# Block-sparse attention and a rational FFN in one pass: four chunks through half of the FFN's units first, and GpSimd's weight loads behind the keys

## The chip, the cores and the metric

The kernel runs on one core of one Trainium2 chip. The metric is the device time of one execution in microseconds (us); lower is better. Engines have the profile's names: PE (TensorE), PEld (its weight loads), DVE (VectorE), ACT (ScalarE), POOL (GpSimd), SP (SyncE, which only issues DMAs).

## What is computed

Four batches of 768 tokens, eight heads of 64, in float32. Attention is sparse by blocks of 32 tokens: a query block sees itself and its two neighbours, the first and the last block, and three sampled blocks; the first and the last query block see all. Its output, 3072 x 512, goes through an FFN whose activation is a rational function:

```python
mask = np.abs(blk_i - blk_j) <= window
mask = mask | (blk_i == 0) | (blk_j == 0) | (blk_i == n_blocks - 1) | (blk_j == n_blocks - 1)
...
attn = attn / (np.sum(attn, axis=-1, keepdims=True) + 1e-09)
...
h = x @ w_in
P = a[0] + a[1] * h + a[2] * h2 + a[3] * h3
Q = 1.0 + np.abs(b[0]) * np.abs(h) + np.abs(b[1]) * h2
g = P / (Q + 1e-06)
return (g @ w_out).astype(np.float32)
```

w_in (512 x 2048) and w_out (2048 x 512) come as 64-bit floats, which no engine computes with: the kernel loads them as pairs of 32-bit words and puts float32 together with integer operations.

## The kernel before, in words

**Chunks, units, parts.** The tokens are cut into 12 chunks of 256, three to a batch. A chunk's FFN has 8 units of 256 hidden features (`unit`, line 1017). A unit is 24 matmuls into hidden features (`into`, lines 1034 to 1036; weights as a float16 high and low half), three activations on ACT, seven operations on DVE that make the rational function (the one that makes its high half, `gh`, is line 1069), and 12 matmuls into the output accumulator (`out_high`, lines 1091 and 1093, and `out_low`, line 1097). Attention (`attention`, line 730) goes by pairs of query blocks, 12 pairs to a batch; the pair with the first and the last block is worked in three parts, so a batch has 14 parts. A part is a group of score matmuls (line 815), four maxima on DVE (827), four exponentials on ACT (846), eight transposes (892) and the products with the values (938). Two pairs make one transposed tile of FFN input (976), four pairs a chunk.

**Near scores.** Batch 0 takes its sampled key blocks out of SBUF: six GpSimd copies a pair (line 759). For that all six key tiles must have been loaded (579), transposed (554) and copied out of PSUM (592).

**Weights.** `weights` (396) loads w_in in 16 pieces of 512 KB (four groups of 512 columns, four pieces each, line 429) and w_out in 16 (426), and decodes each: a conversion on any of three engines, then three operations on DVE (438, 441, 444). A group of w_in also needs a scale, then a scaling and a split into halves; a piece of w_out is copied to `wo_h` (452), its remainder goes to `wo_l` (458), and a bfloat16 copy to `wo_b` (455). GpSimd issues groups 0 and 1 of w_in, SP the rest. Raw pieces of w_in lie in the parts of `wo_l` and `wo_b` that have no weights yet: four places a group (`raw`, 409).

**What sets the order.** Nothing is issued as it is recorded. Every step is an `Op` with an engine, a price, the Ops it waits for and a priority; `issue` (164) then plays a list schedule over the prices and writes one fixed order for each engine. Inside an engine the order is never changed on the chip. An Op may be placed only when its priority is at most 8 above the unit reached. A unit's priority is its place in `order` (393); attention's comes from `part_prio` (1160), a weight piece's from the place of the first unit that needs it. Where the planner sees PE idle at the start, it writes `fill` matmuls there (162), whose result nobody reads. In `order` chunk 0 goes through units 0 to 3, chunk 1 through all 8, then chunk 0 through 4 to 7, and from chunk 2 on each chunk through all 8. Chunk 0's half sum waits in SBUF, in a tile of the ring `r_ld`, and the second half is added to it (1135).

```python
    order = [(0, u) for u in range(HU)] + [(1, u) for u in range(NU)] + [(0, u) for u in range(HU, NU)] + [(c, u) for c in range(2, NC) for u in range(NU)]
```

Of the kernel before, what the change touches and what calls it, by code (L numbers as in the profile page):

```python
# [24 lines left out]
def kernel(  # L25
# [46 lines left out]
    PT = 3  # L72
# [307 lines left out]

    WC = 512
# [4 lines left out]
    wo_b = const.tile([P, NF, DM], BF16, name="wo_b")  # L386
# [6 lines left out]
    order = [(0, u) for u in range(HU)] + [(1, u) for u in range(NU)] + [(0, u) for u in range(HU, NU)] + [(c, u) for c in range(2, NC) for u in range(NU)]  # L393
    place = {cu: n for n, cu in enumerate(order)}

    def weights():
# [5 lines left out]
        for u in range(NG):  # L402
            pieces += [(min(place[0, 2 * u], place[1, 2 * u]) + -4.91, 0, u, x) for x in range(NCC)]
        for x in range(NF):
            pieces.append((min(place[0, x // 2], place[1, x // 2]) + x % 2 / 2 + 0.45, 1, x // NCC, x))
        pieces.sort(key=lambda p: p[0])
        sums, before, begun, freed = {}, [None, None], {}, {}

        def raw(u, x):
            x0 = (x // 2 if u == 0 else 2 + x // 2) * NCC  # L410
            home = [wo_l, wo_b][x % 2][:, x0:x0 + NCC]
            return home.rearrange("p a n -> p (a n)").bitcast(I32)

        def homes(x):
            x //= NCC
            return [freed[0 if x < 2 else NG - 1, 2 * (x % 2) + y] for y in range(2)]

        def one(prio, kind, u, x, before):
            d = {}
            s_wl = Slot(r_wl) if kind else None  # L420
# [39 lines left out]
            wl = [s_wl] if kind else []  # L460
# [6 lines left out]
            o = Op(among("c", SC, sc=520, po=588, ve=335), 0, convert, [o0], prio, takes=w, uses=wl)  # L467
            if not kind:
                begun[u, x] = o
# [5 lines left out]
            if kind:  # L475
                o1 = Op(among("o", SC, sc=520, po=588, ve=335), 0, out_high, [o], prio, uses=w)
                o2 = Op(among("p", PO, po=1225, ve=602), 0, out_low, [o1] + homes(x), prio, uses=w)
                o3 = Op(among("q", SC, sc=520, po=588, ve=335), 0, out_short, [o] + homes(x), prio, uses=w)
                out_ready[x] = [o2, o3]
                decoded.append(o3)  # L480
                decoded.append(o2)
                return o2
# [43 lines left out]
    kall = const.tile([P, NB, HG, BLK], F32, name="kall")  # L526
# [36 lines left out]
    def new_ld(slot):  # L563
        return slot.buf.tile([P, 512], F32, name="ld", bufs=4 if ext and slot.buf is ext[0] else None)
# [44 lines left out]
    def prep(b, when):  # L609
# [9 lines left out]
        def tile_of(w, j):  # L619
            if not first:  # L620
                slot = Slot(r_ld)
                return slot, lambda: new_ld(slot)
            ring, tag, pool = homes[j // 2]
            return Slot(ring), lambda: pool.tile([P, 512], F32, name=tag, bufs={"tt": 3}.get(tag))
# [101 lines left out]
    xbufs = [[const.tile([P, CB, NCC, BLK], F16, name=f"{nm}{e}") for nm in ("xh", "xl")] for e in range(3)]  # L726
# [290 lines left out]
    def unit(c, u):  # L1017

        b, k0 = c // NCH, place[c, u]
        new, last = u == 0 or (c == 0 and u == HU), u == NU - 1 or (c == 0 and u == HU - 1)  # L1020
# [78 lines left out]
        deps = (o_ready[c] + [o_fc[b, u]] if u == 0 else [o_fc[b, u]]) + (in_ready[u * CH // WC] if c < 2 else [])  # L1099
# [17 lines left out]
        wo = out_ready[2 * u] + out_ready[2 * u + 1] if c < 2 else []  # L1117
# [42 lines left out]
    def part_prio(x):  # L1160

        c = next(c for c in range(NC) if x < need[c])
        if c == 0:
            return -19.0 + 1.78 * x
        since, by = place[c - 1, 0], place[c, 0]
        if c == 2:
            since = 9.1
        if c == 1:
            return by + (0.56 * (x + 1 - need[1])) - 1
# [74 lines left out]
```

## Time and profile before

| | |
|---|---|
| three runs | 827.95, 831.24, 833.78 us; median 831.24 |
| the profiled execution | 831.69 us, of which 829.9 us from the first to the last instruction (the span) |
| busy share of the span | PE 93%, DVE 81%, ACT 69%, POOL 12% |
| mean granted clock of PE | 0.981 |
| DMA | 121.30 MB, mean 146 GB/s |

A row of a group has the line, engine, operation, tiles, shapes and count, then the busy time of the group in us, the mean of one in ns, and the idle time of its engine just before it with what ended that. Busy times of matmul groups overlap each other, since each matmul's end is modelled. A granted clock of 1.00 is 2.4 GHz, 0.50 is 1.2 GHz. "issue" as a releaser is a wait whose end the profile can't put down to another instruction.

### The profile page before, as it was taken

To read this page: it belongs to the slowest core of one execution; us is meant where nothing else is said; L and a number is where in the kernel's file an instruction comes from. 1 tells how busy PE (TensorE), PEld (TensorE's weight loads), DVE (VectorE), ACT (ScalarE), POOL (GpSimd) and SP (SyncE) were. 2 spreads that over 40 slices of the span, in tenths; PEclk is the share of its full clock that TensorE was granted. 3 is DMA by queue.
4 is the path that set the end of the run, shared out by engine and by line. 5 is a ranking of instruction groups with operands and counts; after the bars stand their busy time and mean duration, and the time that the engine had idled before them with its cause. 6 is when DMAs were issued, how large, how long until landed. Compare 5 with 4: busy or idle time off the path is not lost.

```text
span 829.9 us, 27531 instructions
## 1 busy us (share of the span) xinstructions
PE 776.0 (93%) x10935; PEld 556.8 (67%) x10935; DVE 673.1 (81%) x1579; ACT 569.9 (69%) x1266; POOL 99.4 (12%) x147
## 2 busy tenths in 40 slices
PE   4997937799899999999999999999999999999997
PEld 2655625676677768677777777677777767767774
DVE  2777899899988985788888884887888886887886
ACT  1775676788777768767576759676676758766563
POOL 1747344533100000000000000000000000000000
PEclk9998977899999999999999999999999999999999
DMA  7877673449555866545536756625556436210000
GB/s 209 239 220 230 193 224 114 138 120 248 154 153 159 203 171 180 166 128 167 147 108 173 188 145 191 181 83 172 149 140 151 116 106 183 77 62 6 1 26 26
DMA packets 224417, 121.30 MB, mean 146 GB/s; under 512 B 62624, under 2 KB 214048, under 8 KB 224288
## 3 DMA queue, kind: packets, MB, share of 16 engines
q1 hardware_dynamic: 223136, 115.34, 50.1%
q0 software_dynamic: 1152, 4.19, 1.4%
q8 instruction: 86, 1.41, 0.7%
q14 instruction: 43, 0.35, 0.1%
HBM read 108.47 MB, written 11.01 MB: 144 GB/s over the span
## 4 chain that ended last, share of the span: by engine, by line
PE 81%; DVE 11%; ACT 3%; issue 3%; SPq 2%; DMA 1%; POOL 0%; ACTq 0%; DVEq 0%
PE acc L1091 10%; PE acc L1093 9%; PE acc L1097 9%; PE ph L1034 9%; PE ph L1035 9%; PE ph L1036 9%; PE m L815 7%; PE av L938 6%; PE m L892 6%; PE acc L162 3%; PE m L554 2%; SPq L579 2%; PE m L976 1%; DVE pr L827 1%; DVE dw L444 1%
## 5 line engine op out<-in xcount | busy, mean ns | idle before, releaser
L1034 PE MATMUL ph<-xh,wi 128*128 128x256 f16 x768 | 210.7, 274 | 1.1 <-DVE tt L1051 1.1
L1035 PE MATMUL ph<-xl,wi 128*128 128x256 f16 x768 | 210.3, 274 | 0.0
L1036 PE MATMUL ph<-xh,wi 128*128 128x256 f16 x768 | 210.3, 274 | 0.0
L1041 ACT ACTIVATE sq<-ph,fc 128x512 f32<-128x512 f32 x96 | 65.9, 686 | 113.4 <-PE ph L1036 113.3
L1091 PE MATMUL acc<-wo_h,gh 128*128 128x512 f32 x384 | 114.4, 420 | 15.5 <-DVE gh L1069 14.8
L846 ACT ACTIVATE pr<-pr,st 128x256 f32<-128x256 f32 x224 | 110.7, 500 | 8.5 <-DVE st L858 8.4
L1058 DVE SCALAR_TENSOR_TENSOR ab<-sq,absb,ab 128x512 f32<-128x512 f32 x96 | 75.6, 787 | 39.0 <-ACT ab L1055 38.5
L1097 PE MATMUL acc<-wo_b,gl 128*128 128x512 bf16 x384 | 99.3, 381 | 4.1 <-DVE gl L1079 4.1
L1093 PE MATMUL acc<-wo_l,gh 128*128 128x512 bf16 x384 | 100.5, 385 | 0.0
L827 DVE CUSTOM_DVE_ANT_1 pr<-m,bias 128x256 f32<-128x256 f32 x224 | 83.5, 419 | 15.4 <-PE m L815 14.9
L150 ACT ACTIVATE pT<-m 128x512 f32<-128x512 f32 x112 | 63.8, 596 | 38.2 <-PE m L892 37.1
L1034 PEld LDWEIGHTS <-wi 128*128 128x128 f16 x768 | 75.9, 99 | 20.5 <-issue 5.4
L1069 DVE SCALAR_TENSOR_TENSOR gh<-tt,par,rr 128x512 fp32r<-128x512 f32 x96 | 72.6, 757 | 19.8 <-ACT rr L1065 11.3
L1091 PEld LDWEIGHTS acc<-wo_h,gh 128*128 128x128 f32 x384 | 66.1, 191 | 28.9 <-POOL wo_l L458 14.6
L1035 PEld LDWEIGHTS <-wi 128*128 128x128 f16 x768 | 75.5, 98 | 12.2 <-issue 0.4
L1036 PEld LDWEIGHTS <-wi 128*128 128x128 f16 x768 | 75.5, 98 | 9.1
L892 PE MATMUL m<-ident,pr 128*128 128x128 f32 x448 | 69.9, 290 | 7.5 <-DVE scw L344 5.1
L1045 ACT ACTIVATE tt<-ph,par,fc 128x512 f32<-128x512 f32 x96 | 74.8, 779 | 0.6 <-DVE gl L1079 0.5
L1075 DVE SCALAR_TENSOR_TENSOR tt<-tt,par,ab 128x512 f32<-128x512 f32 x96 | 74.6, 777 | 0.5
L1048 DVE TENSOR_TENSOR tt<-tt,sq 128x512 f32<-128x512 f32 x96 | 67.1, 698 | 9.4 <-ACT tt L1045 9.4
L892 PEld LDWEIGHTS m<-ident,pr 128*128 128x128 f32 x448 | 63.3, 206 | 16.4 <-ACT ab L1055 5.3
L1055 ACT ACTIVATE ab<-ph,fc 128x512 f32<-128x512 f32 x96 | 65.5, 682 | 12.3 <-DVE tt L1075 11.7
(130 smaller groups left out, 1213.8 us busy)
## 6 DMA issues: line engine op xcount, KB each, us to landing
vg<-in_v_dram SPq DMA_DIRECT2D x312, 64.0 KB, 2.8
vg<-in_v_dram SPq DMA_DIRECT2D x88, 192.0 KB, 3.2
kall<-ks SPq DMA_DIRECT2D x138, 64.0 KB, 1.9
wl<-in_moe_w_out_dram SPq DMA_DIRECT2D x16, 512.0 KB, 4.6
vg<-in_v_dram SPq DMA_DIRECT2D x12, 512.0 KB, 4.9
kall<-ks SPq DMA_DIRECT2D x23, 256.0 KB, 3.2
ldq<-in_q_dram SPq DMA_DIRECT2D x20, 256.0 KB, 3.5
out_dram<-ld SPq DMA_DIRECT2D x20, 256.0 KB, 2.6
```

Source lines behind the costliest of these rows:

```text
L827: nc.vector.tensor_tensor_reduce(out=prs[x][:, e, g].rearrange("p (s r) -> p s r", r=BLK), in0=h["sp"][g][:, e], in1=add.rearrange("p (s o ...
L846: nc.scalar.activation(out=prs[x][:, e, g], in_=prs[x][:, e, g], func=AF.Exp, scale=SCALE, bias=st[:, 12 + y:13 + y], accum_out=st[:, 16 + ...
L892: nc.tensor.transpose(pp[:, jj * P:(jj + 1) * P], pr[:, e, g, kt:NS * BLK:2], ident)
L1034: nc.tensor.matmul(o, wh, xh[:, :, cc], start=(cc == 0), stop=False)
L1035: nc.tensor.matmul(o, wh, xl[:, :, cc], start=False, stop=False)
L1036: nc.tensor.matmul(o, wl, xh[:, :, cc], start=False, stop=(cc == NCC - 1))
L1045: nc.scalar.activation(out=d["tt"], in_=d["ph"], func=AF.Identity, scale=d["cst"][:, 3:4], bias=par[:, 2:3])
L1058: nc.vector.scalar_tensor_tensor(out=d["ab"], in0=d["sq"], scalar=absb[:, 1:2], in1=d["ab"], op0=ALU.mult, op1=ALU.add)
L1075: nc.vector.scalar_tensor_tensor(out=d["tt"], in0=d["tt"], scalar=par[:, 0:1], in1=d["ab"], op0=ALU.add, op1=ALU.subtract)
L1091: nc.tensor.matmul(acc, g, wo_h[:, f], start=(new and e == 0), stop=False)
L1093: nc.tensor.matmul(acc, g, wo_l[:, f], start=False, stop=False)
L1097: nc.tensor.matmul(acc, g, wo_b[:, f], start=False, stop=(last and e == 1))
```

## The change

`order` now starts with chunks 0 to 3, units 0 to 3 of each. Then come units 4 to 7 of chunk 3, then those of chunks 0, 1 and 2. So units 4 to 7, and with them groups 2 and 3 of w_in and pieces 8 to 15 of w_out, are first needed at place 16 (before at place 8). Three chunks keep a half sum, so the ring of `ld` tiles grows from 3 to 7, and a fourth pair of input tiles is added. Space for it comes from `wo_b`, which goes: `out_low` reads the upper 16 bits of each float32 in `wo_h` in its place, a bfloat16 at a step of two. The raw pieces move: groups 0 and 1 of w_in lie in the part of `wi` that groups 2 and 3 will take; groups 2 and 3 share two buffers (`r_wr`), the last quarter of `wo_l` and a tile `wr`. GpSimd's first piece of w_in is held by a one-column copy out of `kall` until the fourth key tile (tokens 384 to 511) has been copied out. Attention of chunks 0 to 2, all of batch 0, has one rising priority from the start.

```diff
@@ the order, and the chunks that share the halves
-    order = [(0, u) for u in range(HU)] + [(1, u) for u in range(NU)] + [(0, u) for u in range(HU, NU)] + [(c, u) for c in range(2, NC) for u in range(NU)]
+    KC = 4
+    order = [(c, u) for c in range(KC) for u in range(HU)] + [(c, u) for c in [KC - 1] + list(range(KC - 1)) for u in range(HU, NU)] + [(c, u) for c in range(KC, NC) for u in range(NU)]
@@ buffers
-    PT = 3
+    PT, LD = 3, 7
...
-    r_ld, r_kt = Ring([p3] * 3), Ring([p1])
+    r_ld, r_kt = Ring([p3] * LD), Ring([p1])
...
+    r_wr = Ring(range(2))
...
-    wo_b = const.tile([P, NF, DM], BF16, name="wo_b")
...
-    xbufs = [[const.tile([P, CB, NCC, BLK], F16, name=f"{nm}{e}") for nm in ("xh", "xl")] for e in range(3)]
+    xbufs = [[const.tile([P, CB, NCC, BLK], F16, name=f"{nm}{e}") for nm in ("xh", "xl")] for e in range(4)]
@@ weights()
-            pieces += [(min(place[0, 2 * u], place[1, 2 * u]) + -4.91, 0, u, x) for x in range(NCC)]
+            pieces += [(min(place[c, 2 * u] for c in range(KC)) + -4.91, 0, u, x) for x in range(NCC)]
...
-                d["ld"] = early.tile([P, 2 * WC], I32, name="wl", bufs=2) if kind else raw(u, x)
+                if kind:
+                    d["ld"] = early.tile([P, 2 * WC], I32, name="wl", bufs=2)
+                elif u < 2:
+                    d["ld"] = wi[:, x, 2:4].rearrange("p u a n -> p (u a n)").bitcast(I32)
+                else:
+                    d["ld"] = wr[s_wl.buf]
...
+                if u == 0 and x == 0:
+                    nc.gpsimd.tensor_copy(out=d["ld"][:, 0:1].bitcast(F32), in_=kall[:, 12, 0, 0:1])
                 (nc.sync if u > 1 else nc.gpsimd).dma_start(out=d["ld"], in_=wi64[r0:r0 + P, u * 2 * WC:(u + 1) * 2 * WC])
...
-                o0 = Op(PO, [(530, 524288)], load, [begun[0, x] if u else k_turned[2]], -17.0 + 1.2 * x if u else -84, behind=before[kind])
+                o0 = Op(PO, [(700, 524288)], load, [k_evac[0][3]] if u == 0 else [freed[0, x]], -17.0 + 1.2 * x if u else -84, behind=before[kind])
...
-                o3 = Op(among("q", SC, sc=520, po=588, ve=335), 0, out_short, [o] + homes(x), prio, uses=w)
-                out_ready[x] = [o2, o3]
+                out_ready[x] = [o2]
@@ unit()
-        new, last = u == 0 or (c == 0 and u == HU), u == NU - 1 or (c == 0 and u == HU - 1)
+        new, last = u == 0 or (c < KC - 1 and u == HU), u == NU - 1 or (c < KC - 1 and u == HU - 1)
...
-                nc.tensor.matmul(acc, g, wo_b[:, f], start=False, stop=(last and e == 1))
+                nc.tensor.matmul(acc, g, wo_h[:, f].bitcast(BF16)[:, 1:2 * DM:2], start=False, stop=(last and e == 1))
@@ part_prio()
-        if c == 0:
+        if c < 3:
             return -19.0 + 1.78 * x
```

The order on POOL at the program's start (`ident` is the identity for transposes, `kx` the sampled key blocks of the first pair), before:

```order
masks.py:197 MEMSET ident 128x128
L305 ISA
L305 IOTA rr 128x24
L429 DMA wo_l<-in_moe_w_in_dram 128x1024
L429 DMA wo_b<-in_moe_w_in_dram 128x1024
masks.py:199 AFFINE_SELECT ident<-ident 128x128
L429 DMA wo_l<-in_moe_w_in_dram 128x1024
L429 DMA wo_b<-in_moe_w_in_dram 128x1024
L709 TENSOR_LOAD ix
L759 ISA
L759 COPY kx<-kall 128x128
```

and now:

```order
masks.py:197 MEMSET ident 128x128
L306 ISA
L306 IOTA rr 128x24
masks.py:199 AFFINE_SELECT ident<-ident 128x128
L432 COPY wi<-kall 128x1
L433 DMA wi<-in_moe_w_in_dram 128x1024 x4
L705 TENSOR_LOAD ix
L755 ISA
L755 COPY kx<-kall 128x128
```

The four loads of group 0 of w_in moved from before every key to behind the wait for the fourth key tile; the first pair's key copies stand right behind them.

The order on DVE ahead of the third `gh` of the program (`wi` rows with `wo_l` or `wo_b` are the decode of w_in's group 2, `dw` rows that of w_out), before:

```order
L444 SCALAR_TENSOR_TENSOR wi<-wo_l,wi 128x512
L438 TENSOR_SCALAR wi<-wi 128x512 x2
L441 SCALAR_TENSOR_TENSOR wi<-wo_b,wi 128x512
L441 SCALAR_TENSOR_TENSOR wi<-wo_l,wi 128x512
L444 SCALAR_TENSOR_TENSOR wi<-wo_b,wi 128x512
L444 SCALAR_TENSOR_TENSOR wi<-wo_l,wi 128x512
L438 TENSOR_SCALAR wi<-wi 128x512
L1058 SCALAR_TENSOR_TENSOR ab<-sq,absb,ab 128x512
L441 SCALAR_TENSOR_TENSOR wi<-wo_b,wi 128x512
L1051 SCALAR_TENSOR_TENSOR tt<-ph,fc,tt 128x512
L444 SCALAR_TENSOR_TENSOR wi<-wo_b,wi 128x512
```

and now, the eleven rows that end with that `gh`:

```order
L442 TENSOR_SCALAR dw<-dw 128x512
L1075 TENSOR_TENSOR gl<-tt,rr 128x512
L445 SCALAR_TENSOR_TENSOR dw<-wl,dw 128x512
L983 SCALAR_TENSOR_TENSOR xl_118<-m_102,xscale,xh_117 128x512
L448 SCALAR_TENSOR_TENSOR dw<-wl,dw 128x512
L1047 SCALAR_TENSOR_TENSOR tt<-ph,fc,tt 128x512
L866 TENSOR_SCALAR st<-st 128x4
L1044 TENSOR_TENSOR tt<-tt,sq 128x512
L960 TENSOR_TENSOR xn<-av,st 128x256
L869 RECIPROCAL st<-st 128x4
L1065 SCALAR_TENSOR_TENSOR gh<-tt,par,rr 128x512
```

The four pieces of group 2 left the place between the second and the third `gh`: the first of them now ends ahead of the sixth `gh`, and between the second and the third stands one piece of w_out.

The order on SP where pieces 2 and 3 of group 3 are loaded (`vg` are value blocks for attention), now, with what each row waits for:

```order
L913 DMA vg_110<-in_v_dram 16x8x128 [waits DMAHW3_49]
L433 DMA wo_l<-in_moe_w_in_dram 128x1024 [waits DMAHW4_49,DVE_49,Pool_49]
L433 DMA wr<-in_moe_w_in_dram 128x1024 [waits DMAHW5_49,DVE_49,Pool_49]
L906 DMA vg_109<-in_v_dram 48x8x128 [waits DMAHW6_49,PE_49]
L913 ISA
L913 DMA vg_109<-in_v_dram 16x8x128 [waits DMAHW7_49]
```

Before, pieces of a group had four places; now two buffers, so a load waits for DVE's decode of the piece two before it, with value loads queued behind on SP.

## Rows read from the trace of the kernel before

**Rows 1.** Busy us (count) of PE, PEld, DVE, ACT, POOL; clock, DMA share, GB/s.

```profile
0.00:96.00 96.00, 77.26 (x1498) 50.89 (x1498) 63.16 (x210) 55.17 (x140) 49.59 (x95) 0.96 0.76 218
96.00:226.00 130.00, 101.80 (x1510) 73.76 (x1510) 126.15 (x271) 95.02 (x216) 49.85 (x53) 0.91 0.59 169
226.00:760.00 534.00, 531.93 (x7512) 388.18 (x7511) 428.66 (x1018) 381.85 (x852) 0.00 (x0) 1.00 0.53 145
760.00:820.00 60.00, 60.00 (x399) 41.67 (x398) 52.25 (x80) 36.75 (x58) 0.00 (x0) 1.00 0.03 10
```

**Rows 2.** PE's waits: us in total, times, longest us.

```profile
PE acc L1091 <- DVE gh L1069: 14.8, 2, 14.4
PE av L938 <- issue: 5.7, 2, 3.9
PE ph L554 <- DMA tt<-in_k_dram: 4.2, 1, 4.2
PE m L815 <- issue: 1.1, 1, 1.1
```

**Rows 3.** DVE in order of time: start us, us, what.

```profile
95.47 0.74 DVE L1069 SCALAR_TENSOR_TENSOR gh<-tt,par,rr 128x512 fp32r<-128x512 f32 x1
109.59 1.09 DVE L444 SCALAR_TENSOR_TENSOR wi<-wo_l,wi 128x512 int32<-128x512 int32 x1
110.61 2.32 DVE L438 TENSOR_SCALAR wi<-wi 128x512 int32<-128x512 int32 x2
126.26 1.09 DVE L1069 SCALAR_TENSOR_TENSOR gh<-tt,par,rr 128x512 fp32r<-128x512 f32 x1
225.30 0.74 DVE L1069 SCALAR_TENSOR_TENSOR gh<-tt,par,rr 128x512 fp32r<-128x512 f32 x1
```

**Rows 4.** Groups by form: three DVE operations that decode a w_out piece.

```profile
L438 DVE TENSOR_SCALAR dw<-dw 128x512 int32<-128x512 int32 x16 | 8.3, 521 | 0.0
L441 DVE SCALAR_TENSOR_TENSOR dw<-wl,dw 128x512 int32<-128x512 int32 x16 | 10.9, 682 | 0.0
L444 DVE SCALAR_TENSOR_TENSOR dw<-wl,dw 128x512 int32<-128x512 int32 x16 | 12.0, 751 | 0.1
```

**Rows 5.** Groups of two lines between 226 and 760 us.

```profile
L1034 PE MATMUL ph<-xh,wi 128*128 128x256 f16 x563 | 153.8, 273 | 0.0
L827 DVE CUSTOM_DVE_ANT_1 pr<-m,bias 128x256 f32<-128x256 f32 x160 | 59.9, 420 | 9.2 <-PE m L815 8.9
```

**Rows 6.** SP in order of time at the start: one row, key loads.

```profile
3.23 9.97 SPq L579 DMA_DIRECT2D ab<-in_k_dram  x2
```

**Rows 7.** DMA issues up to 22 us: count, KB each, median us to landing.

```profile
tt<-in_k_dram SPq DMA_DIRECT2D x2, 256.0 KB, 11.5
sq<-in_k_dram SPq DMA_DIRECT2D x2, 256.0 KB, 4.1
wo_l<-in_moe_w_in_dram POOLq DMA_DIRECT2D x2, 512.0 KB, 8.1
```

**Rows 8.** POOL and PE in order of time at the start.

```profile
1.40 0.74 POOL L429 DMA_DIRECT2D wo_l<-in_moe_w_in_dram  x1 [0.26 <-issue]
27.82 0.54 POOL L429 DMA_DIRECT2D wo_l<-in_moe_w_in_dram  x1
21.59 4.26 PE L162 MATMUL acc<-ident 128*128 128x512 f16 x19
```

**Rows 9.** Groups by form: output matmuls, weight loads, one DVE sum.

```profile
L1091 PE MATMUL acc<-wo_h,gh 128*128 128x512 f32 x384 | 114.4, 420 | 15.5 <-DVE gh L1069 14.8 <-ACT ld L150 0.7
L1097 PE MATMUL acc<-wo_b,gl 128*128 128x512 bf16 x384 | 99.3, 381 | 4.1 <-DVE gl L1079 4.1
L1093 PEld LDWEIGHTS <-gh 128*128 128x128 bf16 x384 | 30.0, 99 | 49.3 <-issue 26.9
L1097 PEld LDWEIGHTS <-gl 128*128 128x128 bf16 x384 | 36.3, 98 | 45.4 <-DVE gl L1079 4.9 <-issue 0.5
L1135 DVE TENSOR_TENSOR ld<-ld,acc 128x512 f32<-128x512 f32 x2 | 1.3, 682 | 0.0
```

More of the change, by code (lines that the diff above doesn't have):

```diff
@@ L378, in bound @@
         nc.scalar.activation(out=scrap[:, :src.free_size()], in_=src, func=AF.Abs, accum_out=mx)
+    kall = const.tile([P, NB, HG, BLK], F32, name="kall")
     WC = 512
@@ L402, in weights @@
         for u in range(NG):
-            pieces += [(min(place[0, 2 * u], place[1, 2 * u]) + -4.91, 0, u, x) for x in range(NCC)]
+            pieces += [(min(place[c, 2 * u] for c in range(KC)) + -4.91, 0, u, x) for x in range(NCC)]
         for x in range(NF):
-            pieces.append((min(place[0, x // 2], place[1, x // 2]) + x % 2 / 2 + 0.45, 1, x // NCC, x))
+            pieces.append((min(place[c, x // 2] for c in range(KC)) + x % 2 / 2 + 0.45, 1, x // NCC, x))
         pieces.sort(key=lambda p: p[0])
[L407 to L412, printed above, removed]
+        sums, before, freed = {}, [None, None], {}
+        wr = [wo_l[:, NF - NCC:].rearrange("p a n -> p (a n)").bitcast(I32), early.tile([P, 2 * WC], I32, name="wr", bufs=1)]
         def homes(x):
-            x //= NCC
-            return [freed[0 if x < 2 else NG - 1, 2 * (x % 2) + y] for y in range(2)]
+            return [freed[NG - 1, y] for y in range(NCC)] if x >= NF - NCC else []
         def one(prio, kind, u, x, before):
             d = {}
-            s_wl = Slot(r_wl) if kind else None
+            s_wl = Slot(r_wl if kind else r_wr) if kind or u > 1 else None
             s_w = Slot(r_dw) if kind else None
             def load():
-                d["ld"] = early.tile([P, 2 * WC], I32, name="wl", bufs=2) if kind else raw(u, x)
+                if kind:
[4 more added lines that the diff above has]
+                    d["ld"] = wr[s_wl.buf]
                 if kind:
@@ L463, in one @@
             else:
-                o0 = Op(PO, [(530, 524288)], load, [begun[0, x] if u else k_turned[2]], -17.0 + 1.2 * x if u else -84, behind=before[kind])
+                o0 = Op(PO, [(700, 524288)], load, [k_evac[0][3]] if u == 0 else [freed[0, x]], -17.0 + 1.2 * x if u else -84, behind=before[kind])
             before[kind] = o0
             w = [s_w] if kind else []
-            o = Op(among("c", SC, sc=520, po=588, ve=335), 0, convert, [o0], prio, takes=w, uses=wl)
-            if not kind:
-                begun[u, x] = o
+            o = Op(among("c", SC, sc=520, po=588, ve=335), 0, convert, [o0] + ([freed[1, x]] if not kind and u > 1 else []), prio, takes=w, uses=wl)
             o = Op(VE, 335, pack1, [o], prio, uses=w)
@@ L563, in new_ld @@
     def new_ld(slot):
-        return slot.buf.tile([P, 512], F32, name="ld", bufs=4 if ext and slot.buf is ext[0] else None)
+        return slot.buf.tile([P, 512], F32, name="ld", bufs=4 if ext and slot.buf is ext[0] else LD)
     def keys(b, t, prio, before, slot, new):
@@ L623, in tile_of @@
             ring, tag, pool = homes[j // 2]
-            return Slot(ring), lambda: pool.tile([P, 512], F32, name=tag, bufs={"tt": 3}.get(tag))
+            return Slot(ring), lambda: pool.tile([P, 512], F32, name=tag, bufs={"tt": 3, "ld": LD}.get(tag))
         before = None
@@ L1116, in unit @@
             s_acc[c] = Slot(r_acc)
[L1117 removed]
+        wo = out_ready[2 * u] + out_ready[2 * u + 1] if c < KC else []
         o = Op(TE, 1690, out_high, [h] + wo, pk[11], behind=chain.get("out"), takes=[s_acc[c]] if new else [], uses=[s_gh] + ([] if new else [s_acc[c]]))
@@ L1162, in part_prio @@
         c = next(c for c in range(NC) if x < need[c])
-        if c == 0:
+        if c < 3:
             return -19.0 + 1.78 * x
         since, by = place[c - 1, 0], place[c, 0]
[L1166 to L1169, printed above, removed]
+        if c < KC:
+            return by + (0.56 * (x + 1 - need[c])) - 1
+        if c == KC:
+            since = place[KC - 1, NU - 1] - 4
         return since + (by - since) * (x + 1 - need[c - 1]) / (need[c] - need[c - 1]) - LEAD
@@ L1195 @@
         b = c // NCH
-        if b == 0 and u % (WC // CH) == 0 and (b, u) not in o_fc:
-            factors(0, u, WC // CH, [scale_ready[u * CH // WC], v_scale[0], o_setup], place[c, u] - 1)
-        elif b and (b, u) not in o_fc:
+        if b < 2 and u % (WC // CH) == 0 and (b, u) not in o_fc:
+            factors(b, u, WC // CH, [scale_ready[u * CH // WC], v_scale[b], o_setup], place[c, u] - 1)
+        elif (b, u) not in o_fc:
             factors(b, 0, NU, [scale_ready[g] for g in range(NG)] + [v_scale[b]], place[c, u] - 2)
```

8 lines of the change are left out of this document (2 added, 6 removed).

## The prediction

> **What bounds the kernel now.** Begin with busy time by stretch [rows 1]. From 226 us to 820 us PE is busy without a break at a granted clock of 1.00 (2.4 GHz): nothing else sets the end there. Before 226 it is not: up to 96 us PE is busy for 77.3, much of it in `fill` matmuls that nobody reads, and from 96 to 226 for 101.8 of 130. In that second stretch DVE is busy for 126.2 of 130, so DVE sets its pace. PE's clock is 0.91 there, a mixture of both levels, 1.2 and 2.4 GHz.
>
> The view of PE's waits names the largest one: 14.4 us in one piece, `out_high` for a `gh` [rows 2]. DVE in order of time says why [rows 3]: between the first `gh` (ends at 96.2) and the third (starts at 126.3) DVE decodes w_in's group 2, whole pieces in a row, because chunk 1 wants units 4 to 7 from place 8 on. The other large waits are 4.2 for the first key tile and 5.7 for value blocks ("issue" at line 938: DMAs that had not landed).
>
> So the end is fixed early. If the thirteenth `gh` (ends at 226.0) is the last one that PE really waited for, the span is 226.0 + 603.9, and whatever lets PE stand further on at such a point comes off the end.
>
> **Unit costs.** The stretch from 760 to 820 holds FFN alone [rows 1]: 399 matmuls at 36 a unit are 11.1 units, so a unit is 60.0/11.1 = 5.41 us of PE and 52.25/11.1 = 4.71 of DVE. From 226 to 760 there are 563/8 = 70.4 units and 160/4 = 40 parts of attention [rows 5]; what is left over is (534 - 381)/40 = 3.8 us of PE and (428.7 - 332)/40 = 2.4 of DVE a part, all its transposes and sums included. A piece of weights costs DVE (8.3 + 10.9 + 12.0)/16 = 1.95 us [rows 4]; I take 2.0 for w_in too. In an FFN-only stretch DVE has 13% to spare; with two decodes to a unit it has none, and attention gives DVE air.
>
> **The change, step by step.** The order is read by engine; each of its rows gets these durations.
>
> *Up to the first gh.* Before it ends at 96.2 [rows 3]. Now 32 more matmul rows (16 transposes, 16 scores) and 3 more fills stand ahead of the first `out_high`: at 60.0/399 = 0.15 us a matmul 4.8, less since scores are small, so 4.0, and 3 x 4.26/19 = 0.7 [rows 8]. Two kinds of waits should go. GpSimd's four loads of 512 KB no longer run beside the six key loads: today the first key tile takes 11.5 us to land, the last 4.1, and SP stands 9.97 us in issuing two of them [rows 6, 7], so I take away the 4.2 us for keys. Of 5.7 + 1.1 us of "issue" waits [rows 2] I take half, since half of w_in now loads much later. First `gh`: 96.2 + 4.0 + 0.7 - 4.2 - 3.4 = 93. With no wait gone it is 101, with all gone 90.
>
> The other side of that move: the first loads wait for the fourth key tile, and the key copies of the first pair stand behind them on POOL, at 0.54 us an issue [rows 8], some 2.7 us with the one-column copy. They wait for the sixth key tile anyway, so I put this at nothing; without that cover it is 2.7. ACT's two first conversions, which now wait for these loads, stand ahead of the first exponentials; a load takes 8.1 us [rows 7], the keys' transposes and the first scores take longer than that today.
>
> *First to ninth gh.* DVE: 8 x 4.71 + 7 x 2.0 + 5.5 x 2.4 + 2 for small ones = 67. PE: 8 x 5.41 + 10 parts (80 transposes) x 3.8 = 81. Here PE is the slower one, which it never was in this stretch before: 7 decodes in place of the 15 ahead of the ninth gh.
>
> *Ninth to twenty-second gh.* The late weights come here. DVE: 13 x 4.71 + 15 x 2.0 + 8.5 x 2.4 + 20 factor operations and some reductions, 6 = 118. PE: 13 x 5.41 + 4 parts x 3.8 = 86. DVE is the slower one again: the pile has moved rather than gone, and is smaller against PE's work.
>
> *Sum.* If the two engines' delays simply added, 81 + 118 = 199; if queues smoothed everything, DVE's 67 + 118 = 185. Before, by the same count, first to thirteenth `gh`: DVE 12 x 4.71 + 20 x 2.0 + 7.5 x 2.4 + 6 = 121, while 130 were taken. So I stay near the upper end: 195. The twenty-second `gh` ends at 93 + 195 = 288. Of PE's work behind the thirteenth `gh` of before, what is now done by that point is the difference of the two orders: 9 units less one `into`, 9 x 5.41 - 2.6 = 46.1, and 48 to 56 transposes with their scores and values, 7 parts x 3.8 = 26.6; together 73. Span: 288 + 603.9 - 73 = 819. The profiled execution took 831.69 against a span of 829.9, 1.8 more, so 821; its own time stands 0.45 above the median of the three runs.
>
> *Costed at nothing.* Sixteen ACT copies to `wo_b` go: ACT is busy 95 of 130 us [rows 1]. Four more sums of half outputs (2 now, 0.68 each [rows 9]) fall where PE is bound and DVE has room; uncovered they are 2.7. The two extra emptyings of the accumulator hide likewise. `out_low`'s strided read: no matmul of before streams bfloat16 at a step of two. The nearest row is the weight load of `gh`, which has that very step and takes 99 ns against 98 without [rows 9], so nothing. The far end is `out_high`, which streams four bytes an element: 114.4 - 99.3 = 15.1 us over 384 matmuls. A gain has no reason.
>
> **A rule that speaks against it.** POOL's rows say that an issue of a weight load took 0.74 us at 1.40, with DVE idle, and 0.54 at 27.82, beside a busy DVE [rows 8]: no penalty, so the sum has none. The Trainium skill, page "SBUF — State Buffer", section "SBUF: two separate sides", has it otherwise: while DVE copies between float32 tiles in SBUF, GpSimd can't write the descriptors of its DMAs, and one of 620 ns takes some 3100; by that figure the four loads, now issued while DVE works, would come 10 us later (an estimate from that page). What such a lock would cost by rows is among the rivals.
>
> **Rivals.**
>
> *More is gained.* Queues smooth the stages (185) and all early waits go (90): 821 - 10 - 3 = 808. For it: the ring of `ld` tiles is longer. Against it: in the 130 us of before DVE lost 9 over its own work.
>
> *Nothing is gained, the pile costs what it did.* Decode in a lump behind the ninth `gh` makes PE wait as the 14.4 us did, DVE's 118 stretch by before's 130/121 to 127, and nothing is smoothed: 81 + 127 = 208, 13 more than I took: 834, within 1%. For it: 15 decodes in 13 units. Against: 20 in 12 before.
>
> *SP is blocked by two buffers (slower).* Groups 2 and 3 load through two buffers in place of four. Six of the eight loads wait on SP for the decode two pieces earlier, and value loads stand behind them in SP's order. If each holds a product back by the longest such wait in the trace, 3.9 us [rows 2], that is 6 x 3.9 = 23: 844. It decides from the point where DVE is later with those decodes than SP's lead over PE. For it: SP has one queue for all. Against: each buffer's next load stands several units ahead of its use, and in 226 to 760 the same queue feeds attention with PE never idle.
>
> *GpSimd's issues are held up by DVE.* If each of the four loads of group 0 waits out two DVE operations at the largest size in [rows 3], 2.32 us for two, they come 9 us later, and since two conversions stand ahead of the first exponentials on ACT, all of attention starts later: 830. Against: the issue of 0.54 us beside a busy DVE.
>
> *The strided read costs* up to its bound, 836; only above 0.05 us a matmul is it slower than before by over 1%.
>
> **How the numbers follow.** My forecast, 821, gets 0.47, with a range of its own from 810 to 830; more gained (808) 0.18; no gain (834) 0.14; SP blocked (844) 0.11; the strided read 0.06, half of it slower; GpSimd held up (830) 0.04. About 1% is what a measurement of this kernel can tell from no change; from 831.24 that is below 823 or above 839.5. Of the forecast's share two thirds lie below 823: 0.31 + 0.18 = 0.49 faster. Slower: 0.11 + 0.03 and a tail of 0.03 of the no-gain case = 0.17. The rest, 0.34, is within 1%. The range leaves out the ends of the first and of the slower rivals: 803 to 840.
>
> **What would show it.** Right: the first `gh` ends between 88 and 98 and the ninth at about 175; no wait over 10 us of `out_high` for `gh` before it; the first key tile is transposed some 4 us sooner than today; PE's last idle stretch ends near the twenty-second `gh`, at 280 to 295; PE's clock between 96 and 226 above 0.91; line 1093 of the changed kernel keeps 0.26 us busy a matmul. Wrong: a first `gh` behind 100; waits of `av` for "issue" over 10 us in total between 175 and 290, which is SP; an `out_low` over 105 us in all; PE idle after 300.

## The result, and the profile after

The changed kernel takes 841.38 us (median of five runs, 840.29 to 850.41), the kernel before 832.32 beside it: a ratio of 1.0142, with a 95% interval from 1.0104 to 1.018. It is 1.4% slower, where 821 us, faster, was forecast. The profiled execution is the longest of the five, 850.41 us with a span of 848.6, 9.0 above the median; so the table of a run near the median, that with a third w_out buffer (experiment 4, 840.17 us profiled), stands beside its own below. Of the ten executions of experiment 2 one took 1957.27 us; without it their median is 831.24 in place of 831.29.

Busy time of the changed kernel by stretch (start:end, length, then busy PE, PEld, DVE, ACT, POOL with counts, PE's granted clock, DMA share, GB/s), to be held against [rows 1]:

```profile
0.00:96.00 96.00, 78.72 (x1546) 52.54 (x1547) 58.17 (x217) 56.30 (x146) 40.45 (x89) 0.97 0.79 208
96.00:226.00 130.00, 110.18 (x1866) 81.35 (x1876) 103.96 (x255) 86.76 (x210) 34.64 (x40) 0.94 0.70 186
226.00:340.00 114.00, 96.34 (x1080) 67.16 (x1090) 98.11 (x198) 75.12 (x160) 29.34 (x23) 0.91 0.55 148
340.00:760.00 420.00, 415.75 (x5684) 304.78 (x5732) 343.31 (x804) 295.51 (x656) 0.00 (x0) 1.00 0.50 139
```

Between 96 and 226 PE does more than before (110.2 us busy for 101.8), as wanted. But the stretch that follows, in which before PE was idle for 1.0 us, now has 17.7 us of gaps at a clock of 0.91 (ten of its matmuls left no record, so a little of that is no gap), and POOL is still at weights.

PE's largest waits after:

```profile
PE m L811 <- issue: 7.0, 4, 2.9
PE acc L1093 <- DVE gl L1075: 6.8, 4, 3.9
PE ph L1030 <- DVE tt L1047: 5.4, 3, 3.5
PE m L550 <- DMA ldq<-in_q_dram: 5.3, 2, 3.0
PE acc L1087 <- DVE gh L1065: 5.2, 4, 3.6
PE av L934 <- issue: 4.5, 2, 3.9
```

The one wait of 14.4 us for a `gh` [rows 2] is gone, and no wait of after is over 4 us; many short ones for DVE's products stand in its place. A list of waits does not show this loss. A table by `gh` does. The first, ninth, thirteenth and twenty-second `gh` on DVE, in order of time, as in [rows 3]:

```profile
89.85 0.74 DVE L1065 SCALAR_TENSOR_TENSOR gh<-tt,par,rr 128x512 fp32r<-128x512 f32 x1
...
174.52 0.75 DVE L1065 SCALAR_TENSOR_TENSOR gh<-tt,par,rr 128x512 fp32r<-128x512 f32 x1
...
237.15 0.74 DVE L1065 SCALAR_TENSOR_TENSOR gh<-tt,par,rr 128x512 fp32r<-128x512 f32 x1
...
313.63 0.74 DVE L1065 SCALAR_TENSOR_TENSOR gh<-tt,par,rr 128x512 fp32r<-128x512 f32 x1
```

Busy time between these four, first of before, then of after:

```profile
96.20:184.40 88.20, 64.31 (x975) 46.74 (x976) 84.92 (x173) 62.28 (x143) 36.69 (x43) 0.86 0.52 154
184.40:226.00 41.60, 37.48 (x537) 27.02 (x535) 41.03 (x100) 32.53 (x75) 12.96 (x10) 1.00 0.73 199
226.00:285.80 59.80, 59.80 (x858) 44.19 (x857) 52.18 (x122) 43.19 (x97) 0.00 (x0) 1.00 0.63 169
```

```profile
90.60:175.30 84.70, 72.10 (x1288) 54.71 (x1297) 67.74 (x161) 58.48 (x142) 23.52 (x31) 0.96 0.68 195
175.30:237.90 62.60, 49.01 (x788) 34.77 (x790) 50.40 (x130) 41.87 (x102) 16.84 (x14) 0.91 0.80 201
237.90:314.40 76.50, 65.66 (x571) 44.03 (x579) 72.28 (x144) 44.51 (x84) 25.03 (x19) 0.89 0.42 112
```

And the same of experiment 4:

```profile
89.10:171.30 82.20, 70.89 (x1287) 52.38 (x1286) 72.58 (x162) 58.52 (x145) 22.99 (x29) 0.96 0.64 184
171.30:224.60 53.30, 47.39 (x742) 33.91 (x746) 42.36 (x113) 39.73 (x93) 10.47 (x10) 0.94 0.73 193
224.60:305.70 81.10, 64.26 (x621) 41.51 (x611) 79.95 (x161) 47.98 (x95) 27.43 (x19) 0.89 0.51 142
```

Before, DVE is idle for 3.3 us up to the ninth `gh` and has all weights behind it at the thirteenth; in the third row PE has no gap. After, DVE is idle for 17.0 of 84.7 us up to the ninth, for 12.2 of 62.6 up to the thirteenth, and then busy for 72.3 of 76.5 with the weights that it did not decode before. In experiment 4 it is 9.6 of 82.2, 10.9 of 53.3, and then 80.0 busy of 81.1. PE is not busy throughout up to the ninth either: it has 72.1 us of 84.7, 70.9 of 82.2 in experiment 4. What DVE waits for most in the changed kernel between the first and the ninth `gh` (us in total, times, longest us) is scores, and GpSimd's conversion of w_out pieces:

```profile
DVE pr L823 <- PE m L811: 8.9, 2, 8.3
DVE dw L442 <- POOL dw L154: 4.5, 2, 4.0
```

Counted by the first of its DVE operations, 14 pieces stand behind the ninth `gh`, 8 between the first and the ninth; before it is 5 and 14.

### The profile page after: what moved, and what is told of

The parts are those of the page before. It is cut to its first block, busy times and chain, and to the rows that moved or that the text cites. A ratio compares the mean times of both kernels' runs of the same rounds, so it can differ in the third digit from the quotient of the medians.

```text
span 848.6 us, 27464 instructions
## 1 busy us (share of the span) xinstructions
PE 783.7 (92%) x10857; PEld 562.7 (66%) x10938; DVE 673.9 (79%) x1588; ACT 563.7 (66%) x1253; POOL 104.4 (12%) x152
## 4 chain that ended last, share of the span: by engine, by line
PE 72%; DVE 8%; SPq 7%; issue 5%; DMA 4%; ACT 3%; POOL 1%; POOLq 0%; ACTq 0%; DVEq 0%
PE acc L1087 9%; PE ph L1030 9%; PE acc L1093 9%; PE ph L1031 8%; PE ph L1032 8%; PE acc L1089 8%; PE m L811 6%; PE av L934 6%; PE m L888 5%; PE acc L162 2%; DMA vg<-in_v_dram 2%; SPq L575 2%; SPq L775 2%; PE m L550 1%; PE m L972 1%
## 5 line engine op out<-in xcount | busy, mean ns | idle before, releaser
L1030 PE MATMUL ph<-xh,wi 128*128 128x256 f16 x768 | 212.8, 277 | 5.4 <-DVE tt L1047 5.4
L1031 PE MATMUL ph<-xl,wi 128*128 128x256 f16 x768 | 212.7, 277 | 0.0
L1032 PE MATMUL ph<-xh,wi 128*128 128x256 f16 x768 | 212.5, 277 | 0.0
L1087 PE MATMUL acc<-wo_h,gh 128*128 128x512 f32 x384 | 116.9, 427 | 5.2 <-DVE gh L1065 5.2
L1093 PE MATMUL acc<-wo_h,gl 128*128 128x512 bf16 x365 | 100.0, 391 | 9.2 <-DVE gl L1075 6.8
L1054 DVE SCALAR_TENSOR_TENSOR ab<-sq,absb,ab 128x512 f32<-128x512 f32 x96 | 72.0, 750 | 29.5 <-ACT ab L1051 29.4
L1089 PE MATMUL acc<-wo_l,gh 128*128 128x512 bf16 x322 | 88.7, 387 | 4.6 <-issue 0.5
L1065 DVE SCALAR_TENSOR_TENSOR gh<-tt,par,rr 128x512 fp32r<-128x512 f32 x96 | 74.2, 773 | 12.9 <-ACT rr L1061 11.5
L1058 ACT ACTIVATE rr<-ab 128x512 f32<-128x512 f32 x96 | 60.7, 633 | 28.0 <-DVE ab L1054 25.7
L934 PE MATMUL av<-vg,pT 128*32 128x64 f32 x3584 | 64.6, 223 | 9.6 <-issue 4.5
```

The costliest lines, as they stand in the source:

```text
L934: nc.tensor.matmul(d["av"][rows, e, g], pT[:, 2 * g + kt, rows], vf[:, head(h4, g), kt * D:(kt + 1) * D], start=(kt == 0 and (n == 1 or (m ...
L1030: nc.tensor.matmul(o, wh, xh[:, :, cc], start=(cc == 0), stop=False)
L1031: nc.tensor.matmul(o, wh, xl[:, :, cc], start=False, stop=False)
L1032: nc.tensor.matmul(o, wl, xh[:, :, cc], start=False, stop=(cc == NCC - 1))
L1087: nc.tensor.matmul(acc, g, wo_h[:, f], start=(new and e == 0), stop=False)
L1089: nc.tensor.matmul(acc, g, wo_l[:, f], start=False, stop=False)
```

## The experiments

Twelve kernels ran in four groups, each against the kernel before on the same chip (its medians there: 831.0, 830.9, 831.1, 830.6 us).

**1. The old order in the new storage.** KC is 2, which is the old order, and part_prio is that of before.

```diff
-    KC = 4
+    KC = 2
```

> The changed kernel with the old order of units (two chunks through the first half, which is the order of before unit for unit) and the old priorities of the attention parts; GpSimd's gate, the two buffers for groups 2 and 3, the strided read and the seven ld tiles stay. Theory O (the order is at fault: batch 1's chunk is wanted at place 12 rather than 24, so its loads, stores and key groups fall among the weights): back to the time of before or under it, 824 to 833, with DVE's wait for group 2 (some 14 us of out_high for gh) back. Theory S (the new storage is at fault: with two buffers SP stands at weight loads while value and key loads queue behind them): still about 840, with SP's waits at weight loads near the 36 us that they are in the changed kernel (15 for w_out and w_in together before).

830.87 us, ratio 0.9998 (0.9975 to 1.0021); the wait for `gh` is back with 12.6 us. The order is at fault; the gate, the new storage and the strided read together cost nothing (experiments 3 and 5 take them apart).

**2. Three chunks.**

```diff
-    KC = 4
+    KC = 3
```

> The changed kernel with three chunks, all of batch 0, through the first half of the units in place of four; nothing else is changed. Theory O: batch 1's attention moves from place 12 to place 24 and takes its loads with it; the late weights are wanted at place 12 in place of 16. 820 to 832, and PE's waits between 96 and 130 us for scores, value products and query tiles are gone. Theory S: 838 to 844, as the buffers are the same.

831.29 us, 0.9997 (0.998 to 1.0014). The fourth chunk alone costs 10.1 us by the two medians, 8.8 when each is taken against the kernel before beside it, and 12 by the ratios. Between 96 and 130 us PE's wait for scores is down to 1.5 us (4.3 in the changed kernel) and those for value products and query tiles are gone, but others stand there, some 10 us in all in place of 6.5; so those waits were not the price.

**3. The gate alone.** The kernel before, with the copy from `kall` and the wait for the fourth key tile in front of GpSimd's loads.

```diff
+                if u == 0 and x == 0:
+                    nc.gpsimd.tensor_copy(out=d["ld"][:, 0:1].bitcast(F32), in_=kall[:, 12, 0, 0:1])
...
-                o0 = Op(PO, [(530, 524288)], load, [begun[0, x] if u else k_turned[2]], -17.0 + 1.2 * x if u else -84, behind=before[kind])
+                o0 = Op(PO, [(530, 524288)], load, [begun[0, x] if u else k_evac[0][3]], -17.0 + 1.2 * x if u else -84, behind=before[kind])
```

> The kernel before with one part of the change: GpSimd's first weight loads wait for the fourth key tile. Both theories: first scores some 5 us sooner than 25.8 us (19.9 in the changed kernel). If the start of attention carries through to the end, 826 to 828; if the first FFN unit waits for something else (its inputs' decode, which starts later now), no change, 829 to 834. A third theory, that the late decode of group 0 is what costs the changed kernel its time, would have 838 to 842 here.

825.32 us, 0.9932 (0.9912 to 0.9952): 5.7 us faster than before, the best kernel of all here. The first scores start at 19.2 us (25.8 before, 19.9 in the changed kernel), and the gain reaches the end.

**4. A third buffer for w_out's pieces.**

```diff
-    PT, LD = 3, 7
+    PT, LD = 3, 6
...
-                    d["ld"] = early.tile([P, 2 * WC], I32, name="wl", bufs=2)
+                    d["ld"] = early.tile([P, 2 * WC], I32, name="wl", bufs=3)
```

> The changed kernel with three buffers in place of two for w_out's pieces on their way in (and six ld tiles in place of seven, for the room). Theory S: SP no longer stands 34 us at these loads, value and key loads come sooner, 828 to 835. Theory O: 837 to 845, since the pieces only land sooner and the decode on DVE is as late.

840.23 us, 1.0134 (1.0102 to 1.0166): no gain. SP's own waits, in the changed kernel and then here, had made these loads suspect:

```profile
SPq L428 <- DVE dw L448: 33.9, 6, 8.0
```

```profile
SPq L428 <- DVE dw L448: 30.1, 5, 12.6
```

The buffer hardly shortened SP's wait, since DVE's decode behind it is what is late. So this run speaks less against theory S than meant. Experiment 2 speaks against it, which has the same two buffers, waits nearly as long for them, and loses nothing against the kernel before:

```profile
SPq L428 <- DVE dw L448: 26.9, 6, 8.6
```

**5. The strided read, with and without the copies.** On top of the gate. In the first run the copies to `wo_b` go, as in the change; in the second they are still made, so that DVE's and ACT's order does not move.

```diff
-                nc.tensor.matmul(acc, g, wo_b[:, f], start=False, stop=(last and e == 1))
+                nc.tensor.matmul(acc, g, wo_h[:, f].bitcast(BF16)[:, 1:2 * DM:2], start=False, stop=(last and e == 1))
```

> The kernel before with GpSimd's gate and with one more part of the change: out_low reads the upper halves of wo_h at a step of two, and the sixteen copies to wo_b go; wo_b stays as a landing place for w_in. Taken against the gate alone (825.3). If the strided read is free, as the prediction had it: 824 to 826. If it costs what the long FFN stretch of the runs so far shows (53.4 us over 200 matmuls against 52.5 over 204, 0.010 us a matmul, 384 of them): 3.7 us more, 828 to 830.

832.15 us, 1.0011 (0.9997 to 1.0026), 6.8 behind the gate and above both ranges.

> The kernel before with GpSimd's gate, and out_low reading the upper halves of wo_h at a step of two; the sixteen copies to wo_b are still made and read by nobody, so that DVE's and ACT's order is that of the gate alone (825.3). If the read costs what its matmuls show (88.4 us in all against 85.6): 828 to 829. If the whole 6.8 us by which the run without the copies was behind the gate come from the read: 831 to 833. If from the order, which moves when ACT's copies go: the rest, about 4 us, is not seen here.

829.08 us, 0.9977 (0.9953 to 1.0002). So by the medians the read costs 3.8 us and the order that moves when the copies go another 3.1; the two intervals touch, so the second is loose. The group of `out_low` with the gate alone, and with the read at a step of two:

```profile
L1099 PE MATMUL acc<-wo_b,gl 128*128 128x512 bf16 x384 | 99.6, 382 | 2.4 <-DVE gl L1081 2.4
```

```profile
L1099 PE MATMUL acc<-wo_h,gl 128*128 128x512 bf16 x384 | 103.3, 390 | 3.9 <-DVE gl L1081 3.9
```

Busy time grows by 103.3 - 99.6 = 3.7 us, which is all of the read's share. The run without the copies has one long wait on PE, for an ACT copy of keys, that the gate alone does not have; whether it is the 3.1 us is not shown:

```profile
PE m L892 <- ACT kt L150: 13.9, 1, 13.9
```

**6. The gate with three chunks**, in the old storage.

```diff
-    order = [(0, u) for u in range(HU)] + [(1, u) for u in range(NU)] + [(0, u) for u in range(HU, NU)] + [(c, u) for c in range(2, NC) for u in range(NU)]
+    KC = 3
+    order = [(c, u) for c in range(KC) for u in range(HU)] + [(c, u) for c in [KC - 1] + list(range(KC - 1)) for u in range(HU, NU)] + [(c, u) for c in range(KC, NC) for u in range(NU)]
```

> The kernel before with GpSimd's gate and the order of units with three chunks through the first half (four ld tiles, four landing places as before, wo_b as before). If the three-chunk order is worth nothing by itself, as it was beside the new storage: 823 to 828, like the gate alone. If it was only held back by the two landing buffers: 815 to 821, better than both kernels.

827.19 us, 0.9959 (0.9932 to 0.9985): not better than the gate alone, so the landing buffers did not hold the order back.

**7. No unit waits for batch 1.** The FFN of the fourth chunk and of the later ones reads the activations of the chunk before, and their attention is due one chunk later.

```diff
-                xh, xl = xs_of[c]
+                xh, xl = xs_of[c - (c > 2)]
```

> The changed kernel with the FFN of the fourth chunk and of those after it reading the activations of the chunk before (so chunk 2's twice, and the last chunk's attention is read by nobody): the same work and the same order of units, but no unit waits for batch 1 before place 32. Theory O1 (the wait of place 12 for batch 1's attention, with its chain of loads, stores and softmax, leaves both engines idle between the ninth and the thirteenth gh): ninth to thirteenth gh takes 25 to 35 us in place of 62.6, DVE is idle for under 6 us between the ninth and the twenty-second gh in place of 16, and the time is 820 to 828. Theory O2 (DVE's decode in a lump is the loss, batch 1 or not): ninth to twenty-second gh stays over 130 us, and the time is 835 to 842.

842.4 us, 1.014 (1.0116 to 1.0165). Between the four `gh`:

```profile
88.30:180.00 91.70, 74.28 (x1198) 53.76 (x1199) 71.29 (x157) 65.97 (x156) 21.86 (x28) 0.93 0.69 205
180.00:203.80 23.80, 22.21 (x153) 15.71 (x152) 23.80 (x39) 16.39 (x29) 8.87 (x8) 1.00 0.18 51
203.80:282.80 79.00, 60.20 (x605) 40.11 (x604) 78.77 (x145) 47.03 (x93) 29.34 (x23) 0.91 0.39 107
```

The second row does what theory O1 said, 23.8 us with DVE never idle, and yet nothing is gained: the third is still 79.0 long, with DVE busy for 78.8 and PE for 60.2. Both theories miss a part, O1 its time, O2 its stretch. What the two kernels share is the third row. The twenty-second `gh` ends at 282.8 us in place of 314.4, but 556.2 us of the span follow it in place of 534.2, since attention of batch 1 is still to be done there; up to it PE is idle for 37.8 us, 37.0 in the changed kernel.

**8. Two of three decode operations left out of the late weights.**

```diff
-            o = Op(VE, 602, pack2, [o], prio, uses=wl + w)
-            o = Op(VE, 602, pack3, [o], prio, uses=wl + w)
+            if kind == 0 and u < 2 or kind and x < NF // 2:
+                o = Op(VE, 602, pack2, [o], prio, uses=wl + w)
+                o = Op(VE, 602, pack3, [o], prio, uses=wl + w)
```

> The changed kernel without two of the three decode operations of w_in's groups 2 and 3 and of the second half of w_out (the low bits and the sign of these weights are left out): 32 DVE operations at some 0.7 us, 22 us of DVE less between the ninth and the twenty-second gh. Theory O1: the stretch from ninth to thirteenth gh hardly moves (55 to 62 us), and the time falls by what the later pile loses, 825 to 832. Theory O2: the whole 22 us come off, 815 to 821.

829.67 us, 0.9987 (0.9968 to 1.0007): 11.7 of the 22 us come off the time. The third stretch falls from 76.5 to 62.0 us, the second only to 56.1. Both signs are those of theory O1, and O2's time is missed:

```profile
174.60:230.70 56.10, 46.82 (x745) 33.57 (x743) 43.92 (x115) 40.93 (x98) 19.80 (x21) 0.93 0.76 189
230.70:292.70 62.00, 57.85 (x601) 39.36 (x602) 60.91 (x121) 36.70 (x71) 20.56 (x17) 0.95 0.53 144
```

That DVE's work in the third stretch is paid in the time is what both theories share; how much is due to batch 1 is left to the next three runs.

**9. The late decode due four places earlier.**

```diff
-        pieces += [(min(place[c, 2 * u] for c in range(KC)) + -4.91, 0, u, x) for x in range(NCC)]
+        pieces += [(min(place[c, 2 * u] for c in range(KC)) + -4.91 - 4 * (u > 1), 0, u, x) for x in range(NCC)]
...
-        pieces.append((min(place[c, x // 2] for c in range(KC)) + x % 2 / 2 + 0.45, 1, x // NCC, x))
+        pieces.append((min(place[c, x // 2] for c in range(KC)) + x % 2 / 2 + 0.45 - 4 * (x >= NF // 2), 1, x // NCC, x))
```

> The changed kernel with the decode of w_in's groups 2 and 3 and of the second half of w_out due four places earlier: by the order 14 pieces stand ahead of the ninth gh on DVE in place of 8, 8 behind it in place of 14. Theory L (the late lump on DVE is the loss: between the thirteenth and the twenty-second gh DVE is busy for 72.3 of 76.5 us, while it is idle for 17 of 84.7 ahead of the ninth): thirteenth to twenty-second gh falls to 58 to 66 us, the first to the ninth stays under 92, and the time is 829 to 835. Theory O1 (batch 1's attention, wanted at place 12, is the loss): ninth to thirteenth gh stays over 52 us and the time at 836 to 842.

834.42 us, 1.0011 (0.9981 to 1.0041): 7.0 us of the 10.1 come back from a change in due times alone (5.7 with each kernel against the kernel before beside it). The due times also move the loads and with them the planner's order of other instructions.

```profile
88.30:188.30 100.00, 83.69 (x1446) 62.10 (x1448) 89.48 (x198) 72.84 (x178) 35.96 (x40) 0.95 0.73 211
188.30:234.70 46.40, 39.21 (x662) 28.33 (x657) 44.77 (x121) 31.46 (x76) 19.61 (x19) 0.96 0.75 196
234.70:296.60 61.90, 55.79 (x556) 37.38 (x550) 58.03 (x116) 38.42 (x70) 7.57 (x6) 0.97 0.43 112
```

The third stretch falls to 61.9 as theory L had it, and the second under 52, against O1. The first grew to 100.0, more than L's 92: the decode is paid there now. The time from the first to the twenty-second `gh` is 208.3 in place of 223.8.

**10. Batch 1 at place 16.** Three chunks, then chunk 3 ahead of the second halves of chunks 0 and 1.

```diff
-    KC = 4
-    order = [(c, u) for c in range(KC) for u in range(HU)] + [(c, u) for c in [KC - 1] + list(range(KC - 1)) for u in range(HU, NU)] + [(c, u) for c in range(KC, NC) for u in range(NU)]
+    KC = 3
+    order = [(c, u) for c in range(KC) for u in range(HU)] + [(c, u) for c in [KC - 1] for u in range(HU, NU)] + [(3, u) for u in range(NU)] + [(c, u) for c in range(KC - 1) for u in range(HU, NU)] + [(c, u) for c in range(4, NC) for u in range(NU)]
...
```

> The changed kernel with three chunks, all of batch 0, through the first half, then the second half of chunk 2, then all of chunk 3 (batch 1's first) and only then the second halves of chunks 0 and 1: batch 1 is wanted at place 16 (12 in the changed kernel, 24 with three chunks and the chunks in turn), the late weights at place 12. Theory O1: batch 1 wanted early costs wherever it stands, 836 to 842, with both engines idle ahead of the seventeenth gh. Theory L: the weights come as with three chunks, so the time does too, 829 to 833.

833.93 us, 1.0037 (1.0018 to 1.0056): 2.6 above three chunks in turn, just past L's bound and under O1's. Batch 1 wanted early costs something, but little.

**11. Batch 1's parts four places earlier.**

```diff
-            return by + (0.56 * (x + 1 - need[c])) - 1
+            return by + (0.56 * (x + 1 - need[c])) - 5
```

> The changed kernel with batch 1's parts of attention for place 12 (and with them its loads) due four places earlier. Theory O1, if the loss is that this chain of loads, stores and softmax is started too late to be hidden: ninth to thirteenth gh falls from 62.6 to under 45 us, and the time to 830 to 836. If its loads collide with the weights', whenever they come: first to ninth gh grows by what the next stretch gains, 838 to 846.

836.82 us, 1.006 (1.0042 to 1.0079), between the two. Ninth to thirteenth `gh` takes 39.4 us, first to ninth 103.2, thirteenth to twenty-second still 75.6, all of it DVE's. By its order 12 pieces in place of 8 now stand between the first and the ninth `gh`, so its gain can't be put to batch 1 alone.

## Why the prediction was wrong

**The parts, by medians.** Gate: 831.0 to 825.3, -5.7. Strided read: +3.8. Copies gone: +3.1. New landing places and `ld` tiles: 832.2 to 830.9. Three chunks and the new priorities: 830.9 to 831.3. The last two are within what the intervals allow for nothing. Fourth chunk: +10.1, to 841.4. What the gate gave, the strided read and the order without the copies took, and the order of units for which room was made had a price where it was to have a gain.

**The step that failed** is "Ninth to twenty-second gh", with the sum that rests on it. It took DVE's 118 us, less 4 for queues that smooth the stages, so 114 from the ninth (forecast for 174, came at 175.3) to 288. It took 139.1. Of the 25 us more, 4 are the smoothing that did not come, 4.7 are DVE's work (122.7 busy for 118), and 16.4 are DVE standing idle, 12.2 of them between the ninth and the thirteenth `gh`. In experiment 4, near the median, it is 134.4: 4 of smoothing, 4.3 of work, 12.1 idle. The other steps of that run nearly cancel out, so these 20.4 us are the whole miss (840.2 for 821). Experiments 7, 9 and 11 each took most of the idle time between the ninth and the thirteenth away, which gave back -1.0, 7.0 and 4.6 us; the most came where the third stretch shrank too.

So the runs put in its place: **the deferred decode is most of the loss, some 7 of the 10.1 us** by experiment 9. Up to the thirteenth `gh` DVE is idle for 29.2 us (20.6 in experiment 4, 12.2 in experiment 9, 3.9 before); that time is not had again, because behind it DVE has the late pieces beside FFN units that keep it busy for 4.71 us of PE's 5.41 each. The step saw that the pile moved; it did not charge for the decode that the idle DVE left undone. Batch 1's early chunk is a smaller part, 2.6 us by experiment 10, and the two together, 9.6, nearly make the 10.1; they were taken from different orders, so this is a fair agreement and no proof. The orders in one list, with the place at which the late weights are due and the place at which batch 1 is wanted: 16 and 12, 841.4 us (changed kernel); 12 and 12, 834.4 (experiment 9); 12 and 16, 833.9 (experiment 10); 12 and 24, 831.3 (experiment 2).

PE's clock may have a part in this that no run takes by itself. Between the first and the twenty-second `gh` it is 0.92 in the changed kernel and 0.93 in experiment 4, 0.96 in experiments 2 and 9. Over the whole span PE is idle for 53.0 us and busy for 785.1 in experiment 4, 47.4 and 781.8 in experiment 2: of 8.9 us between these two spans, 3.3 are longer work and not waiting.

**Point by point.**
- First `gh`: forecast 93, came at 90.6. The first key tile is turned at 6.2 us (13.6 before), 7.4 sooner where 4 was said. The terms offset each other: ahead of the first `gh` the wait for the first key tile fell by 2.7 us (4.2 to 1.5) where 4.2 was taken, the "issue" waits by 1.1 (6.8 to 5.7) where 3.4 was; a wait of the first fill for `ident`, 6.2 us before and 1.7 now, was not in the sum. Nor were the two "issue" waits of `av` in the kernel before for value blocks, as the prediction read them: they end 1.3 and 1.4 us after a DMA of instructions (last section), so the 3.9 us with which it priced a blocked SP is no wait for SP either. The gate's cost on POOL, put at nothing, is nothing: four issues in 2.34 us, and the key copies behind them still wait 1.92 us for DVE's copy of the keys.
- First to ninth `gh`: 81 forecast from PE's work, 84.7 taken, DVE 67 forecast, 67.7 busy. The time is right and DVE's work too, but PE's work is not: it is busy for 72.1 us (70.9 in experiment 4), and the rest is waiting that the step had no term for. So the 81 is partly luck. PE's clock from 96 to 226 is 0.94, above 0.91 as said.
- Behind the twenty-second `gh`: forecast 819 - 288 = 531 us, taken 848.6 - 314.4 = 534.2, and 532.4 in experiment 4. The count of PE's work moved ahead (73 us) holds; what is too much is about what the strided read costs the 74 units that are left, 2.9 us (an estimate, 74/96 of the 3.8).
- PE's last idle stretch was to end at 280 to 295; PE still waits for a `gh` at 328.
- The strided read, costed at nothing between bounds of 0 and 15.1, is 3.8. The nearest row taken, a weight load with that step, misled: it costs a load nothing (99 ns for 98) and a moving operand 8 ns a matmul (390 for 382). Half of the chance of this rival was called slower than 839.5, though its far end was 836. That line 1093 "keeps 0.26 us" is a miss by 0.01: between 380 and 760 us of the kernel with three chunks 200 of them are busy for 53.4 us, where 204 of before were for 52.5.
- ACT's copies to `wo_b`, costed at nothing because ACT has room, cost some 3.1 us by going: the order of the other instructions moves when they are not there. That is shown by two runs; which instruction it hangs on is not.

**The rivals.** "Nothing is gained, the pile costs what it did" named the mechanism, at 834 us, and was held for 14 in 100. "SP is blocked" gave 844, near the result by another way: of the wait for the two buffers of groups 2 and 3 that it rests on, no row of a microsecond or more is in SP's waits of the changed kernel (in experiment 7 it is 20.1 us), and the old order with the same buffers loses nothing. "GpSimd's issues are held up" falls. Its premise, issues while DVE works, did not come about: the four of group 0, from 11.41 to 13.75, lie in 4.00 us in which DVE waits for PE. One of group 1, at 30.41, does lie beside a DVE operation:

```profile
11.41 2.34 POOL L433 DMA_DIRECT2D wi<-in_moe_w_in_dram  x4 [0.32 <-POOL wi L432]
...
30.41 0.54 POOL L433 DMA_DIRECT2D wi<-in_moe_w_in_dram  x1
```

```profile
14.83 0.69 DVE L152 COPY kall<-ph 128x512 f32<-128x512 f32 x1 [4.00 <-PE ph L550]
...
30.34 0.69 DVE L448 SCALAR_TENSOR_TENSOR wi<-wi 128x512 int32<-128x512 int32 x1
```

The issue at 30.41 lies wholly inside a DVE operation from SBUF to SBUF and takes 0.54 us, as the issues beside an idle DVE do (2.34 for four). The trace does not show the 3100 ns of the Trainium skill's page "SBUF — State Buffer", section "SBUF: two separate sides"; but this operation is not the copy of which the page tells that, so the page is not tested by it.

## What to carry to other kernels

Work that must be done once before a steady stage, here the decode on DVE, does not shrink when its consumers are put off: ask for each stretch which engine idles, and if it is the one that owes the deferred work, charge that idle time at the end. A sum of the slower engine by stretch leaves out the time in which that engine waits for the other, here 12.1 to 16.4 us of DVE, and it can come out right by luck where both wait. When one change carries several edits, one run with the smallest of them alone may already be the best version; here the gate by itself is 0.7% faster than before.

## What was not expected of the hardware

A bfloat16 operand that is streamed into a matmul at a step of two elements takes 390 ns a matmul of 512 columns for 382 packed, 3.7 us over 384, while the same step in a weight load shows no cost [rows 9]. And PE stops in the middle of one product of small matmuls for "issue", with no instruction as the cause: 7.0 us in four gaps of scores in the changed kernel, 1.1 in one before [rows 2]. The DMA records of the traces have what ends them. One queue brings instructions in packets of 16 KB, 86 of them in the changed kernel (packets, MB, share of 16 engines):

```profile
q8 instruction: 86, 1.41, 0.7%
```

In the fourteen traces PE has 54 "issue" gaps of half a microsecond or more between 10 and 330 us, in scores, value products and units, and every one ends 1.2 to 1.6 us after the end of such a packet; the one of 2.86 us from 104.80 to 107.66 follows a packet from 105.35 to 106.31, and the 16 DMA engines are busy throughout. So by the order in time PE waits there for its own instructions; no run tests it. These gaps are 11.5 us in the changed kernel and 10.0 in experiment 4, 6.8 before and 6.5 in experiment 2, so a part of the fourth chunk's price may lie here; DVE's longest wait for scores, 8.3 us, spans the gap of 2.86.
